# Attention sums moved between engines, centring and decoding split otherwise, in a fused attention and gating kernel

## The chip, the cores and the metric

The kernel runs on one core of one Trainium2 chip. The metric is the device time of one execution in microseconds; the median of the runs is compared. A core has five engines with instruction streams of their own: TensorE (PE) for matrix products, whose weight loads stand in the profile as PEld, VectorE (DVE), ScalarE (ACT), GpSimd (POOL) and SyncE (SP), which issues most of the transfers. The engines wait for each other through semaphores alone.

## The reference

Four batches, twelve heads, 448 positions, 64 columns a head. A capped attention is followed by a block with a gate over positions. Every output has to be there in fp32.

```python
scores = cap * tanh(q @ k.T / sqrt(64) / cap)
attn = exp(scores - max(scores))
attn = attn / (sum(attn) + 1e-09)
x = (attn @ v)                      # heads side by side: 448 x 768
h = gelu_tanh(x @ w_in)             # 768 x 1024
u, v = h[..., :512], h[..., 512:]
v_n = (v - mean(v)) / sqrt(var(v) + 1e-06) * g_ln
v_s = einsum('ts,bsd->btd', w_sg, v_n) + b_sg[None, :, None]
out = x + (u * v_s) @ w_out         # 512 x 768
```

## The kernel before

**Matrix products.** The large products run in a one-pass fp32 format; to keep the precision, each operand is split into a high and a low half, and a product is three matmuls (high times high, high times low, low times high: `TERMS`). Score products use the same split of q and k (`split`, lines 506 and 513), except for head pairs marked in `PLAIN`. The weights come as 64-bit floats and are decoded on the chip, chunk by chunk (`decode`: five steps named low, high, shift, sign and whole, of which the last is an addition on GpSimd, then high and low half).

**Attention.** A batch is three groups of two head pairs. A group has seven units: three key chunks of 128 for each of the two pairs, and one unit with the last 64 keys of both. Each unit is a score step on PE (lines 524, 532, 540), a tanh and an exp on ScalarE (595, 597) and a value step on PE (556, 566). The tiles of exponentials `p` come out of a pool of five, the PSUM tiles of scores `sc` out of two. The denominator, the sum of exponentials over all keys, is made on PE: a matmul against a matrix with one column of ones (`den_op`, line 455) adds a tile of exponentials into the tile `den`. Two units go into one operation of four matmuls. The table `SUMS` says for each of the twelve groups how much VectorE adds up beforehand (`add`, line 608): 0, nothing, and seven units go to PE; 1, the three chunks of each pair are added on VectorE (four additions), and two sums and the tail tile go to PE as three units; 2, the tail tile is added too, in two additions of 64 partitions, and two units are left. After a batch, `recip` sends `den` through DRAM, takes the reciprocal and spreads it; `norm` (675) multiplies the head outputs by it.

**The gated block.** `gated(b)` runs on a finished batch: `hv` (line 729) and `hu` (767) are the two halves of the product with W_in, `vsg` (784) that over positions, `outp` (804) that with W_out. `hv` takes GELU (710 to 717), mean and variance (739, 740), the power -1/2 on GpSimd (743), then the layer norm as one VectorE instruction with two columns, mean and factor (745), and then splits the result into halves (`cop` at 300 or 302, `sub` at 328). The bias (789) multiplies by `g_ln` and adds `b_sg`. `outp` ends with the residual (814) and a store (817).

**Order.** Nothing schedules at run time. Every piece of work is an operation of the class `Plan`; `ORDER` is a table of numbers written out by hand or by a planner, and `Plan.run` emits the operations in that order, so it sets the order on every engine. The last bit of each number chooses the engine where an operation is declared for both VectorE and ScalarE (`BOTH`). PE works on a batch's attention and an earlier batch's gated block by turns.

## Time and profile before

| | |
|---|---|
| median of 3 runs | 376.49 us (376.44 to 376.51) |
| the profiled execution | 376.32 us |
| its span, first to last instruction | 374.5 us |
| busy: PE, VectorE, ScalarE, GpSimd | 369.3, 302.4, 211.6, 39.7 us |
| denominator matmuls (line 455) | 160 records, 19.9 us |
| additions of exponentials (line 608) | 48, 53.9 us |

A busy share is the time in which an engine has at least one instruction running. PE's matmuls overlap, and their ends are modelled, so the starts are what can be read closely: the chain of waits shows each piece from its start to the start of what follows. A matmul in plain fp32 appears as two records, one in the one-pass format as one. VectorE instructions overlap a little too, so the chain's pieces of VectorE are shorter than the mean duration in a group.

### The profile page before, as it was taken

The page shows a single profiled execution, that of the slowest core. Times are in us where ns is not written, and L with a number is a line of the kernel's source. Part 1 is how long each engine was busy: PE and PEld are TensorE (multiplying, and loading weights), DVE is VectorE, ACT ScalarE, POOL GpSimd, SP SyncE. Part 2 cuts the span into 40 slices and gives each one's busy share as a digit, 9 for nine tenths or more (in the row PEclk, how much of TensorE's full clock was granted, in tenths as well). Part 3 has the DMA queues.
Part 4 walks back from the last instruction along what each step waited for, and adds up shares of the span by engine and source line. Part 5 has one row for each costly group of instructions (what it writes and reads, how often), then busy time and mean ns, then how long its engine had stood idle before and what let it go on. Part 6 is the DMA issues. An engine that isn't in the chain of part 4 may idle for free.

```text
span 374.5 us, 5508 instructions
## 1 busy us (share of the span) xinstructions
PE 369.3 (99%) x2064; PEld 251.3 (67%) x2064; DVE 302.4 (81%) x559; ACT 211.6 (56%) x275; POOL 39.7 (11%) x39
## 2 busy tenths in 40 slices
PE   8999999999999999999999999999999999999995
PEld 3334343454877587446478976476889999889995
DVE  2899999999989999989795779889366988438763
ACT  5999999995675758797914377751031411033200
POOL 0321121500311412020000100000001000002000
PEclk9999999999999999999999999999999999999999
DMA  7899164455381245146520021202120101400004
GB/s 264 296 274 309 67 200 139 108 168 149 96 259 44 61 118 194 43 119 201 166 80 2 14 79 42 80 3 78 31 79 24 45 6 51 172 2 0 2 0 172
DMA packets 23130, 39.65 MB, mean 106 GB/s; under 512 B 5472, under 2 KB 17728, under 8 KB 23104
## 3 DMA queue, kind: packets, MB, share of 16 engines
q1 hardware_dynamic: 22816, 38.96, 33.4%
q8 instruction: 16, 0.26, 0.3%
q10 hardware_dynamic: 288, 0.34, 0.3%
q14 instruction: 10, 0.08, 0.1%
HBM read 33.28 MB, written 6.02 MB: 105 GB/s over the span
## 4 chain that ended last, share of the span: by engine, by line
PE 82%; DVE 9%; DMA 3%; ACT 2%; issue 2%; SPq 1%; DVEq 0%; ACTq 0%
PE ps L556 12%; PE ps L767 11%; PE ps L729 10%; PE ps L804 10%; PE sc L524 9%; PE ps L784 8%; PE sc L804 6%; PE den L455 3%; PE sc L767 3%; DMA n<-spread 3%; PE sc L729 2%; PE sc L532 2%; PE ps L566 2%; DVE p L608 2%; SPq L320 1%
## 5 line engine op out<-in xcount | busy, mean ns | idle before, releaser
L597 ACT ACTIVATE p<-p,cap 128x896 f32<-128x896 f32 x84 | 84.8, 1040 | 0.7
L595 ACT ACTIVATE p<-sc 128x896 f32<-128x896 f32 x63 | 56.5, 912 | 15.8 <-DVE p L608 7.1
L556 PE MATMUL ps<-p,v 128*64 128x448 f32 x288 | 61.3, 551 | 0.0
L608 DVE TENSOR_TENSOR p<-p,p 128x896 f32<-128x896 f32 (+1 forms) x48 | 53.9, 1132 | 5.1 <-PE ps L556 2.7
L729 PE MATMUL ps<-winv,rg 128*128 128x512 f32 x205 | 50.8, 394 | 0.0
L524 PEld LDWEIGHTS sc<-hl 64*128 64x128 f32 x378 | 32.7, 185 | 26.0 <-ACT p L595 11.9
L767 PE MATMUL ps<-rg,winu 128*128 128x448 f32 x223 | 49.7, 363 | 0.0
L524 PE MATMUL sc<-hl 64*128 64x448 f32 x378 | 48.5, 384 | 0.0
L767 PEld LDWEIGHTS ps<-rg,winu 128*128 128x128 f32 x223 | 41.8, 188 | 4.0 <-issue 0.7
L729 PEld LDWEIGHTS ps<-winv,rg 128*128 128x128 f32 x205 | 38.5, 188 | 8.6 <-issue 0.7
L400 POOL TENSOR_TENSOR stage<-stage 128x512 int32<-128x512 int32 (+1 forms) x20 | 30.2, 1513 | 113.5 <-DVE stage L395 58.8
L556 PEld LDWEIGHTS ps<-p,v 128*64 128x64 f32 x288 | 17.5, 136 | 34.1 <-issue 21.9
L710 ACT ACTIVATE t<-ps 128x448 f32<-128x448 f32 (+1 forms) x25 | 14.2, 566 | 45.6 <-PE ps L729 29.5
L804 PE MATMUL ps<-rg,wout 128*128 128x448 f32 x166 | 39.4, 366 | 0.0
L804 PEld LDWEIGHTS ps<-rg,wout 128*128 128x128 f32 x166 | 30.8, 188 | 5.0 <-issue 2.7
L784 PE MATMUL ps<-wsg,rg 128*128 128x448 f32 x130 | 30.4, 367 | 0.0
L715 ACT ACTIVATE t<-t 128x448 f32<-128x448 f32 (+1 forms) x30 | 18.0, 602 | 21.5 <-DVE t L712 21.5
L743 POOL TENSOR_TENSOR sm<-sm,pw 128x1 f32<-128x1 f32 x14 | 8.7, 627 | 186.8 <-DVE sm L741 177.4
L784 PEld LDWEIGHTS ps<-wsg,rg 128*128 128x128 f32 x130 | 24.0, 188 | 3.8 <-issue 1.0
L712 DVE SCALAR_TENSOR_TENSOR t<-t,ps 128x448 f32<-128x448 f32 (+1 forms) x25 | 16.2, 649 | 12.6 <-ACT t L710 12.4
L804 PE MATMUL sc<-rg,wout 128*128 128x448 f32 x98 | 24.1, 363 | 0.0
L595 ACT ACTIVATE p<-sc,qsc 128x896 f32<-128x896 f32 x21 | 20.9, 1005 | 4.8 <-PE den L455 1.6
(117 smaller groups left out, 469.0 us busy)
## 6 DMA issues: line engine op xcount, KB each, us to landing
raw<-in_qk_dram SPq DMA_DIRECT2D x22, 448.0 KB
stage<-in_w_in_dram SPq DMA_DIRECT2D x12, 512.0 KB
n<-spread SPq DMA_DIRECT2D x24, 224.0 KB
out_dram<-x SPq DMA_DIRECT2D x23, 224.0 KB
v<-in_vp_dram SPq DMA_DIRECT2D x24, 192.0 KB
stage<-in_w_out_dram SPq DMA_DIRECT2D x8, 384.0 KB
u<-in_w_sgT_dram SPq DMA_DIRECT2D x4, 224.0 KB
vt<-in_vt_dram SPq DMA_DIRECT2D x12, 64.0 KB
```

Source lines behind the costliest of these rows:

```text
L400: nc.gpsimd.tensor_tensor(out=a.bitcast(I32), in0=a.bitcast(I32), in1=hi, op=ALU.add)
L524: nc.tensor.matmul(out=sc.t[:, h, :S], lhsT=hl[s].t[rows, w, 1, 128 * c - 128:128 * c], rhs=hl[s].t[rows, m, 0], start=(k == 0), stop=(k = ...
L556: nc.tensor.matmul(out=pav[s].t[64 * h:64 * h + 64, :S], lhsT=v[s].t[:, 128 * (c - 1) + 64 * h:128 * (c - 1) + 64 * h + 64], rhs=p.t[:, h, ...
L595: op(name("tanh", s, c), "act", c_act(2 * S, True, raw_scores), lambda p=p, sc=sc, r=raw_scores: nc.scalar.activation(out=p.t, in_=sc.t[:, ...
L597: op(name("exp", s, c), "act", c_act(2 * S, False, True), lambda p=p: nc.scalar.activation(out=p.t, in_=p.t, func=ACTF.Exp, scale=cap_sb), ...
L608: op(name("add", s, t), "dve", c_tt(2 * S), lambda: nc.vector.tensor_tensor(out=a.t[rows], in0=a.t[rows], in1=p.t[rows], op=ALU.add), rd=[ ...
L712: op(tag + " cube", "dve", c_tt(n), lambda: nc.vector.scalar_tensor_tensor(out=view(), in0=view(), scalar=1.0 / GELU_A, in1=src(), op0=ALU ...
L715: op(tag + " tanh", "act", c_act(n), lambda: nc.scalar.activation(out=view(), in_=view(), func=ACTF.Tanh, scale=GELU_C * GELU_A), wr=[sq])
L729: nc.tensor.matmul(out=ps.t[:, :HF], lhsT=(xl if a else xh)[c].t[:, t * 128:t * 128 + 128], rhs=win[w][1][:, c, :], start=(c == 0 and k == ...
L767: nc.tensor.matmul(out=ps.t[:, :S], lhsT=win[w][0][:, c, f * 128:(f + 1) * 128], rhs=(xl if a else xh)[c].t[:, :S], start=(c == 0 and k == 0),
L784: nc.tensor.matmul(out=ps.t[:, :S], lhsT=(vl if a else vh)[c].t[:, f * 128:(f + 1) * 128], rhs=wsg[w][:, c, :], start=(c == 0 and k == 0), ...
L804: nc.tensor.matmul(out=ps.t[:, :S], lhsT=wout[w][:, f, c * 128:(c + 1) * 128], rhs=(gl if a else gh)[f].t[:, :S], start=(f == 0 and k == 0 ...
```

## The change

- `SUMS`: group 4 goes from 0 to 1, groups 5, 6 and 7 from 1 to 2. (A further value, 3, gets code and is not used.)
- The layer norm becomes two steps. `center` subtracts the mean and multiplies by -1; it may run on VectorE or ScalarE and needs the mean alone. The factor is applied where the halves are made (`both`): the high half is the centred tile times the factor column, on VectorE or ScalarE, and the low half is the same product minus the high half, in one VectorE instruction. The bias multiplies by the negated `g_ln` (`gneg`, made once), which undoes the -1.
- The decoding step high may run on ScalarE too.
- The stores of the pairs in `LANES` (the last of batch 2 and five of batch 3) are issued in two halves.
- The bias tile lies between the v columns of W_in and W_sg in SBUF; some small tiles move.
- `ORDER` is a new table.

```diff
-SUMS = (0, 1, 1, 1, 0, 1, 1, 1, 2, 2, 2, 2)
+SUMS = (0, 1, 1, 1, 1, 2, 2, 2, 2, 2, 2, 2)
+LANES = (17, 18, 19, 20, 21, 22)
 ORDER = (
-    14, 0, 336, 338, 340, 344, 6, 342, 4, 10, 8, 16, 348, 350, 2, 32, 420, 358, 352, 360, 372, 364, 366, 354, 380, 18,
+    16, 0, 338, 340, 342, 344, 6, 346, 4, 10, 8, 18, 422, 352, 2, 34, 350, 360, 354, 50, 366, 362, 374, 368, 356, 382,
...
+    bsg_sb = wp.tile([128, S], FP32, name="bsg_sb")
+    wsg = [wp.tile([128, NC, S], FP32R, name=f"wsg{w}") for w in range(2)]
...
+    op("gneg", "dve", 0.15, lambda: nc.vector.tensor_scalar(
+        out=gneg, in0=g_sb, scalar1=-1.0, scalar2=None, op0=ALU.mult), rd=[k_const], wr=[k_neg])
...
-        def high_bits():
+        def high_bits(e):
             _, hi, a = words()
-            nc.vector.tensor_scalar(out=a, in0=f32(hi), scalar1=2.0 ** -112, scalar2=None, op0=ALU.mult)
+            if e == "dve":
+                nc.vector.tensor_scalar(out=a, in0=f32(hi), scalar1=2.0 ** -112, scalar2=None, op0=ALU.mult)
+            else:
+                nc.scalar.activation(out=a, in_=f32(hi), func=ACTF.Copy, scale=2.0 ** -112)
...
-            op(name("layernorm", t), "dve", 0.55, lambda: nc.vector.tensor_scalar(
-                out=vv(), in0=vv(), scalar1=sm.t[:, 6:7], scalar2=sm.t[:, 0:1],
-                op0=ALU.subtract, op1=ALU.mult), rd=[sm], wr=[v2])
+            def center(e):
+                if e == "dve":
+                    nc.vector.tensor_scalar(
+                        out=vv(), in0=vv(), scalar1=sm.t[:, 6:7], scalar2=-1.0, op0=ALU.subtract, op1=ALU.mult)
+                else:
+                    nc.scalar.activation(out=vv(), in_=vv(), func=ACTF.Identity, scale=-1.0, bias=sm.t[:, 6:7])
+
+            def both(tag, rows, hi, lo, rd, wr_hi, wr_lo):
+                def high(e):
+                    if e == "dve":
+                        nc.vector.tensor_scalar(out=hi(), in0=v2.t[rows, :HF], scalar1=sm.t[rows, 0:1], scalar2=None, op0=ALU.mult)
+                    else:
+                        nc.scalar.activation(out=hi(), in_=v2.t[rows, :HF], func=ACTF.Copy, scale=sm.t[rows, 0:1])
...
+                op("%d v%s lo %d" % (b, *tag), "dve", c_tt(HF) + 0.06, lambda: nc.vector.scalar_tensor_tensor(
+                    out=lo(), in0=v2.t[rows, :HF], scalar=sm.t[rows, 0:1], in1=f32(hi()), op0=ALU.mult, op1=ALU.subtract),
...
-                out=tt.t[:, :S], in0=ps.t[:, :S], scalar=g_sb[:, f:f + 1], in1=bsg_sb, op0=ALU.mult, op1=ALU.add),
-               rd=[ps, k_const, k_bsg], wr=[tt])
+                out=tt.t[:, :S], in0=ps.t[:, :S], scalar=gneg[:, f:f + 1], in1=bsg_sb, op0=ALU.mult, op1=ALU.add),
+               rd=[ps, k_neg, k_bsg], wr=[tt])
...
-                op(name("store", c) + "ab"[n], eng, ISSUE, lambda sl=sl, queue=queue: queue.dma_start(
-                    out=outT[b, c][:, sl], in_=x.t[:, sl]), rd=[(x, sl.start)], size=128 * cols * 4)
+                parts = 2 if not last and b * KD + c in LANES else 1
+                for m in range(parts):
+                    sm = slice(sl.start + cols * m // parts, sl.start + cols * (m + 1) // parts)
+                    op(name("store", c) + "abc"[n + m + (parts > 1)], eng, ISSUE, lambda sl=sm, queue=queue: queue.dma_start(
+                        out=outT[b, c][:, sl], in_=x.t[:, sl]), rd=[(x, sl.start)], size=128 * cols // parts * 4)
```

Three places show what the new table does. Lines of the changed program are higher by about ten: 556, 524, 532, 455 on PE are 566, 534, 542, 465 there, and 506, 513, 608 on VectorE are 516, 523, 618.

On PE, in batch 1, where the second group (group 4) ends and the third begins. Before, tiles of exponentials go to the denominator one by one:

```order
L524 MATMUL sc0_132<-hl1_90 128x448 x6
L524 MATMUL sc1_133<-hl0_89 128x448 x6
L455 MATMUL den_146<-p2_98,const_sb_79 32x448 x2
L455 MATMUL den_146<-p1_97,const_sb_79 32x448 x2
L532 MATMUL sc0_132<-raw1_87 64x448 x2
L532 MATMUL sc0_132<-raw2_88 64x448 x2
L455 MATMUL den_146<-p0_96,const_sb_79 32x448 x2
L455 MATMUL den_146<-p3_99,const_sb_79 32x448 x2
L524 MATMUL sc1_133<-hl0_89 128x448 x6
L524 MATMUL sc0_132<-hl0_89 128x448 x6
```

The same place now:

```order
L534 MATMUL sc1_134<-hl0_90 128x448 x6
L542 MATMUL sc0_133<-raw1_88 64x448 x2
L542 MATMUL sc0_133<-raw2_89 64x448 x2
L566 MATMUL ps1_136<-p3_100,v0_92 64x448 x2
L566 MATMUL ps1_136<-p4_101,v0_92 64x448 x2
L534 MATMUL sc1_134<-hl0_90 128x448 x6
L465 MATMUL den_147<-p0_97,const_sb_80 32x448 x2
L465 MATMUL den_147<-p2_99,const_sb_80 32x448 x2
L534 MATMUL sc0_133<-hl0_90 128x448 x6
```

One operation of the denominator stands here instead of two; the tiles it reads are sums that VectorE has made.

On VectorE, at about the same place, from the reciprocal of batch 0 (the tile `d`) on. Before:

```order
L641 SCALAR_TENSOR_TENSOR d0_145<-d0_145,guard_70 64x84
L644 RECIPROCAL d0_145<-d0_145 64x84
L395 SCALAR_TENSOR_TENSOR stage3_83<-stage3_83 128x512
L395 SCALAR_TENSOR_TENSOR stage1_81<-stage1_81 128x512
L300 CAST winv0_71<-stage2_82 128x512
L386 TENSOR_SCALAR stage0_80<-stage0_80 128x512
L513 SCALAR_TENSOR_TENSOR hl0_89<-raw1_87,root_69,hl0_89 128x832
L300 COPY x7_108<-ps2_136 128x448
L390 TENSOR_SCALAR stage0_80<-stage0_80 128x512
L328 TENSOR_TENSOR winv1_72<-stage2_82,winv0_71 128x512
```

Now:

```order
L664 RECIPROCAL d0_146<-d0_146 64x84
L516 TENSOR_SCALAR hl0_90<-raw1_88,root_70 128x832
L618 TENSOR_TENSOR p0_97<-p0_97,p4_101 128x896
L523 SCALAR_TENSOR_TENSOR hl0_90<-raw1_88,root_70,hl0_90 128x832
L405 SCALAR_TENSOR_TENSOR stage2_83<-stage2_83 128x512
L516 TENSOR_SCALAR hl1_91<-raw2_89,root_70 128x832
L618 TENSOR_TENSOR p0_97<-p0_97,p1_98 128x896
L400 TENSOR_SCALAR stage1_82<-stage1_82 128x512
L303 CAST winu0_63<-stage0_81 128x512
L303 COPY x8_110<-ps0_135 128x448
L618 TENSOR_TENSOR p2_99<-p2_99,p3_100 128x896
L618 TENSOR_TENSOR p2_99<-p2_99,p4_101 128x896
```

Four additions stand between the reciprocal and the normalisation where decoding stood before.

On VectorE, at the start, after the first scalars. `stage` are the tiles of weights being decoded, `hl` those of the score split. Before:

```order
L513 SCALAR_TENSOR_TENSOR hl0_89<-raw1_87,root_69,hl0_89 128x832
L380 TENSOR_SCALAR stage0_80<-stage0_80 128x512
L386 TENSOR_SCALAR stage1_81<-stage1_81 128x512
L386 TENSOR_SCALAR stage0_80<-stage0_80 128x512
L390 TENSOR_SCALAR stage0_80<-stage0_80 128x512
L395 SCALAR_TENSOR_TENSOR stage0_80<-stage0_80 128x512
L506 TENSOR_SCALAR hl1_90<-raw2_88,root_69 128x832
```

Now:

```order
L523 SCALAR_TENSOR_TENSOR hl0_90<-raw1_88,root_70,hl0_90 128x832
L394 TENSOR_SCALAR stage0_81<-stage0_81 128x512
L387 TENSOR_SCALAR stage0_81<-stage0_81 128x512
L400 TENSOR_SCALAR stage0_81<-stage0_81 128x512
L405 SCALAR_TENSOR_TENSOR stage0_81<-stage0_81 128x512
L516 TENSOR_SCALAR hl1_91<-raw2_89,root_70 128x832
L523 SCALAR_TENSOR_TENSOR hl1_91<-raw2_89,root_70,hl1_91 128x832
L394 TENSOR_SCALAR stage1_82<-stage1_82 128x512
```

The first instruction on the second weight chunk (`stage1`) has moved from ahead of the rest of the first chunk to behind it and behind the next score split.

## Rows read from the trace of the kernel before

**Rows 1.** The page's first part: busy us (share of the span) and instructions of each engine.

```profile
PE 369.3 (99%) x2064; PEld 251.3 (67%) x2064; DVE 302.4 (81%) x559; ACT 211.6 (56%) x275; POOL 39.7 (11%) x39
```

**Rows 2.** Busy time by stretch: length, each engine, clock, DMA share, GB/s.

```profile
60.00:80.00 20.00, 20.00 (x148) 8.14 (x144) 19.21 (x28) 19.52 (x22) 6.77 (x4) 1.00 0.39 103
80.00:100.00 20.00, 20.00 (x101) 12.43 (x98) 19.50 (x36) 12.41 (x19) 1.31 (x1) 1.00 0.48 154
```

**Rows 3.** What PE waited for: us in total, times, longest.

```profile
PE ps L355 <- PEq L891: 0.8, 1, 0.8
```

**Rows 4.** Chain of waits, PE pieces: start, us until the next, line, records.

```profile
10.18 0.89 PE den L455 x8
...
12.49 0.90 PE ps L556 x4
...
17.72 1.65 PE ps L556 x8
19.37 1.43 PE sc L524 x12
20.80 1.64 PE den L455 x16
...
32.50 0.80 PE sc L524 x6
```

**Rows 5.** Chain of waits from 44 to 112 us, VectorE pieces.

```profile
75.75 0.53 DVE x L300
...
76.81 0.34 DVE winu L300
...
78.82 0.30 DVE r L300
79.12 1.01 DVE p L608
...
90.55 0.56 DVE hl L506
...
92.14 1.00 DVE hl L513
93.14 0.54 DVE rg L328
93.68 0.53 DVE wsg L328
```

**Rows 6.** PE in order of time, 80 to 104 us: start, us, records.

```profile
90.08 5.09 PE L729 MATMUL ps<-winv,rg 128*128 128x512 f32 x21
95.00 0.62 PE L729 MATMUL ps<-winv,r 128*128 128x512 f32 x2
```

**Rows 7.** What VectorE waited for up to 130 us.

```profile
DVE stage L386 <- DMA stage<-in_w_in_dram: 2.7, 2, 1.8
DVE hl L506 <- DMA raw<-in_qk_dram: 2.3, 1, 2.3
```

**Rows 8.** VectorE groups by shape: busy us, mean ns, idle before.

```profile
L608 DVE TENSOR_TENSOR p<-p,p 128x896 f32<-128x896 f32 x40 | 45.2, 1142 | 0.8 <-PE ps L556 0.3
...
L745 DVE TENSOR_SCALAR t<-t,sm 128x512 f32<-128x512 f32 x14 | 7.7, 557 | 2.2 <-POOL sm L743 2.1
...
L300 DVE CAST rg<-t 128x512 fp32r<-128x512 f32 x11 | 4.6, 421 | 0.2
```

**Rows 9.** ScalarE groups by shape: the tanh of the GELU.

```profile
L715 ACT ACTIVATE t<-t 128x512 f32<-128x512 f32 x14 | 8.8, 631 | 12.8 <-DVE t L712 12.8
```

**Rows 10.** VectorE in order of time, 50 to 64 us: one addition.

```profile
53.01 2.20 DVE L608 TENSOR_TENSOR p<-p,p 128x896 f32<-128x896 f32 x1
```

**Rows 11.** GpSimd in order of time, 44 to 64 us: the addition of a decoding.

```profile
52.57 1.68 POOL L400 TENSOR_TENSOR stage<-stage 128x512 int32<-128x512 int32 x1 [5.52 <-DVE stage L390]
```

**Rows 12.** Stores on SP: ns min/median/max, first and last start.

```profile
L817 SPq DMA_DIRECT2D out_dram<-x x24: 332/422/570, 160.3 to 371.4; - x24
```

**Rows 13.** Chain of waits from 366 us: the last matmuls, the last residual.

```profile
368.83 1.82 PE sc L804 x9
370.65 0.02 issue
370.67 0.39 DVE x L814
```

More of the change, by code (lines that the diff above doesn't have):

```diff
@@ L250, in tiles, with small @@
         return [wp.tile(shape, dtype, name=f"{name}{i}") for i in range(n)]
-    win = [[wp.tile([128, KD, HF], FP32R, name=f"winu{w}")] for w in range(2)]
-    wout = tiles(2, [128, KF, DM], FP32R, "wout")
-    cap_sb = wp.tile([128, 1], FP32, name="cap")
-    qsc = wp.tile([128, 1], FP32, name="qsc")
-    root = wp.tile([128, 1], FP32, name="root")
-    guard = wp.tile([128, 1], FP32, name="guard")
-    for w in range(2):
-        win[w].append(wp.tile([128, KD, HF], FP32R, name=f"winv{w}"))
-    wsg = tiles(2, [128, NC, S], FP32R, "wsg")
+    def small(n, name):
+        return wp.tile([128, n], FP32, name=name)
+    win = [[None, None], [None, None]]
+    for w in range(2):
+        win[w][0] = wp.tile([128, KD, HF], FP32R, name=f"winu{w}")
+    wout = [wp.tile([128, KF, DM], FP32R, name=f"wout{w}") for w in range(2)]
+    gneg, cap_sb, qsc, root = small(KF, "gneg"), small(1, "cap"), small(1, "qsc"), small(1, "root")
+    for w in range(2):
+        win[w][1] = wp.tile([128, KD, HF], FP32R, name=f"winv{w}")
+    bsg_sb = wp.tile([128, S], FP32, name="bsg_sb")
+    wsg = [wp.tile([128, NC, S], FP32R, name=f"wsg{w}") for w in range(2)]
     sms = tiles(4, [128, 8], FP32, "sm")
@@ L445, in attention @@
         per = {}
-        total = sum((NU, 3, 2)[s] for s in SUMS[NG * b:NG * b + NG])
+        total = sum((NU, 3, 2, 1)[s] for s in SUMS[NG * b:NG * b + NG])
         def den_op(units):
@@ L622, in group, with fold @@
                     add(per[s], p, c)
+                if SUMS[g] == 3:
+                    if c == FC:
+                        def fold(s=s, src=per[s], dst=per[0]):
+                            nc.vector.tensor_tensor(
+                                out=dst.t[64 * s:64 * s + 64], in0=src.t[:64], in1=src.t[64:], op=ALU.add)
+                        op(name("fold", s), "dve", c_tt(2 * S), fold, rd=[per[s]], wr=[per[0]], fast=True)
+                    if (s, c) == (1, FC):
+                        add(per[0], tail_p, 0)
+                        den_unit(pairs[0], 1, per[0], last)
+                    continue
                 if SUMS[g] == 2 and (c == 0 or (s, c) == (1, 1)):
@@ L738, in hv @@
             sm = Buf(sm_p)
-            op(name("stats", t), "dve", 0.69, lambda: nc.vector.bn_stats(out=sm.t[:, 0:6], in_=vv()), rd=[v2], wr=[sm])
-            op(name("mean", t), "dve", 0.18, lambda: nc.vector.bn_aggr(out=sm.t[:, 6:8], in_=sm.t[:, 0:6]), wr=[sm])
+            op(name("stats", t), "dve", 0.69, lambda: nc.vector.bn_stats(out=sm.t[:, 0:6], in_=vv()), rd=[v2], wr=[(sm, "r")])
+            op(name("mean", t), "dve", 0.18, lambda: nc.vector.bn_aggr(out=sm.t[:, 6:8], in_=sm.t[:, 0:6]),
+               rd=[(sm, "r")], wr=[(sm, "m")])
@@ L755, in hv @@
                 mine, other = slice(TL * n, TL * n + TL), slice(TL - TL * n, 2 * TL - TL * n)
[L756 to L758 removed]
+                both((" tail", n), mine, lambda h=h, m=mine: h.t[m], lambda h=h, o=other: h.t[o], [v2], (h, 0), (h, 1))
         uu = {}
```

27 lines of the change are left out of this document (14 added, 13 removed), and 156 rows, old and new, of the table ORDER.

## The prediction

> **What bounds the kernel now.** I read the engines' shares first, then busy time by stretch, then what TensorE's idle time was, and then the chain of waits for the price of each kind of work. TensorE (PE) is busy 369.3 of 374.5 us, VectorE (DVE) 81% [rows 1]. A busy share alone does not say that PE is the bound, so the next views matter more: in the stretches the granted clock is 1.00, PE has no idle time from 60 to 100 us [rows 2], and the largest idle wait of PE in the whole span is 0.8 us, ahead of its first instruction [rows 3]. The chain of waits gives the distance from one start to the next, and this distance is the same each time: a lone denominator operation (eight records, four matmuls) takes 0.89 us and two in a row 1.64, so 0.75 each and 0.14 for entering that kind of work; a lone value step 0.90 and two 1.65, so 0.75 and 0.15; score steps 0.80 and 1.43, so 0.63 and about 0.18 [rows 4]. With such fixed distances the stream of PE is a sum that can be written down, and what is taken out of it shortens the end by as much, provided that the other engines still deliver in time. That proviso is the second half of the reading: VectorE is busy 19.2 and 19.5 of 20 us from 60 to 100, ScalarE 19.5 of 20 from 60 to 80 [rows 2]. In the first half PE is dense because VectorE just keeps up.
>
> The Trainium skill, "Perfetto Trace Analysis", section Identifying the Most-Contended Engine, says that matmul busy time is a poor measure and that the share of weight loads should be looked at. By it the 67% of PEld would mean that PE has room, and the time would stay where it is. The fixed distances in [rows 4] speak against that here; the rival is priced below.
>
> **What leaves PE.** A denominator unit is one tile of exponentials that PE sums over its partitions; two units make one operation. Per group of two head pairs SUMS 0, 1, 2 means 7, 3, 2 units. Batch 0 stays at 7+3+3 = 13 units; batch 1 goes from 3+7+3 = 13 to 3+3+2 = 8; batch 2 from 3+3+2 = 8 to 2+2+2 = 6; batch 3 stays at 6. In operations (an odd unit costs one by itself): 7+7+4+3 = 21 before, 7+4+3+3 = 17 after. Four leave: 4 x 0.75 = 3.00 us, and 4 x 0.89 = 3.56 if each stood alone [rows 4].
>
> **What the new order adds to PE.** I counted in both programs how often PE enters a kind of work: scores 35 before and 37 after, values 32 and 35, denominators 18 and 16; tails and plain scores are unchanged. That is 2 x 0.18 + 3 x 0.15 - 2 x 0.14 = +0.53 us. All other matmuls are the same in number and size. Net on PE: -3.00 + 0.53 = **-2.47 us**.
>
> **What VectorE gets.** Ten more additions, 48 to 58 (the four of group 4, and two half-partition ones each in groups 5, 6, 7), 1.01 us each by distance [rows 5]. Against that seven of 14 centrings, five of 21 high halves of the score splits and nine decoding steps go to ScalarE, so over the whole run VectorE's work grows by only 1 or 2 us. But the place decides. I take the last low half of batch 0's normalised activations, the row at 93.14 us [rows 5], which the first projection (hv) waits for. Counting the VectorE instructions ahead of it in both programs: 6 more additions (+6.06), one score split less (-0.56 - 1.00), two evacuations of PSUM less (-1.06), two decoding steps and one high half of W_in less, of one size (3 x 0.34 = -1.02), two high halves of the activations more (+0.60), and two chunks of W_sg split now on VectorE (+0.60 + 1.06) [rows 5]. Sum **+4.7 us** of work ahead of that instruction, while PE's stream up to the same matmul is about as long as before: three of the four removed operations stood ahead of it, but two plain score steps of batch 2 and some projection steps now do.
>
> How much of this has cover? In the kernel before, the low half ends at 93.7. The projection run of PE starts at 90.08 [rows 6]; 21 of its matmuls take 4.92 us up to the next row's start at 95.00, 0.23 each; six steps of three stand ahead of the step that reads the low half in its third matmul, (18 + 2) x 0.23 = 4.6, so it is wanted at about 94.7: 1.0 us of slack. Second, VectorE waited 2.7 us for two W_in loads early on [rows 7], and the new order has a score split and the rest of chunk 0 in those places, so I count these 2.7 us as regained. The 2.3 us for the first qk load [rows 7] stay; its second half is issued one place earlier, ahead of a v load, which gains at most one issue. 4.7 - 1.0 - 2.7 = **1.0 us** by which PE waits. Bounds: nothing, if the rest is absorbed too; 3.7, if nothing of the early waits is regained. I take 1.0.
>
> Centring now needs only the mean, not the power that GpSimd computes; that takes the short wait on GpSimd out of VectorE's way in front of the centring, and puts it in front of the high half. The high half on VectorE now takes the factor from a column: between a cast of that size, 421 ns, and the centring with two such columns, 557 ns [rows 8]; ten of them, so 0 to 1.4 us, only half of them before 130 us. I take the upper price, and it stays inside the bounds above. A centring on ScalarE lies near its 631 ns for a tile of that size [rows 9]. From 80 us on ScalarE has gaps (12.4 of 20 us busy) [rows 2], which cover the centrings at no cost; before 80 us it has next to none, and gets a few decoding steps, each of which makes an exponential later by its own length. I count that into the same bounds. The negated gain column is one column wide; the bias tile's new address changes no instruction: both at nothing, and the rows show no time that hangs on an address.
>
> **GpSimd beside the additions.** A 2.20 us addition instead of 1.14 stands in the trace, beside a GpSimd addition of 1.68 us that began 0.44 us before it [rows 8, 10, 11]. GpSimd has the same 20 decoding additions in both programs, so I add nothing for it.
>
> The Trainium skill, "SBUF — State Buffer", says that a VectorE instruction with two SBUF inputs and a GpSimd instruction that reads SBUF exclude each other, and the later one blocks for the whole of the other. The pair in [rows 10, 11] agrees. By that rule the loss goes by the number of GpSimd instructions, not of additions, and the sum keeps its zero; read from the row alone, each of the ten additions could lose 1.1 us, and the sum would come out slower than before.
>
> **The end.** Six stores of the end become twelve; an issue on SP takes 0.33 to 0.57 us, median 0.42 [rows 12]. After the matmuls of the last whole residual (c = 1), PE still has four steps of three matmuls, 0.20 each (2.4 us) [rows 13], and SP has four or five halves to issue (1.7 to 2.1), so the queue is just free when the last residual is done. Taken at 0; bounds -0.3 (less data in flight behind the last store) and +0.6.
>
> **Sum.** The profiled execution took 376.32 us with a span of 374.5; the median is 376.49. -2.47 + 1.0 = -1.47: span 373.0, and against the median **375.0 us**.
>
> **Rivals.** (a) *VectorE fully keeps up*: no wait arises, 376.49 - 2.47 = 374.0; with 3.56 for the four operations 373.5 (-3.56 + 0.53). For it: the order was rebuilt around the new work, and centring has left VectorE's chain. Against: VectorE busy 19.5 of 20 us. (b) *VectorE is late, slower than before*: the additions of groups 4 and 5 hold tiles of exponentials (five buffers) and stand ahead of the normalisation of batch 0 and of the next score splits; if the early waits come back in another place, PE waits 4.7 - 1.0 = 3.7 us, 376.49 - 2.47 + 3.7 = 377.7. It turns slower from 2.47 us of PE waits. For it: [rows 2] and the 1.0 us of slack. (c) *The change does not reach the end*: what leaves PE comes back as waits of the same size, or PE had room all along; 376.5. (d) *The end grows*: SP's queue holds the last store back by 0.6 on top of the forecast, 375.6.
>
> **How the numbers follow.** Forecast 0.45, (a) 0.18, (b) 0.20, (c) 0.09, (d) 0.08. A change of 0.2% (0.75 us) is about what a measurement here can tell from none: faster below 375.74, slower above 377.24. The forecast (374.2 to 375.9) gives 0.41 faster and 0.04 same; (a) is faster; (b), spread from 376.5 to 378.2, gives 0.15 slower and 0.05 same; (c) 0.01 faster, 0.07 same, 0.01 slower; (d) 0.02 faster, 0.06 same. Together 0.62, 0.22, 0.16. The range leaves out half of (b) and the edge of (a): 373.6 to 377.4.
>
> **What would show it.** In the trace of the changed kernel the denominator's records should fall from 160 to 132, each lone operation still 0.89. PE's starts should be as evenly spaced as now, with one or two holes between 60 and 150 us that end with VectorE, about 1 us in all; VectorE's early wait on W_in loads should be gone. Holes of 3 us or more, or ScalarE waiting on additions for its tiles, is (b); no hole is (a). The end now comes 3.8 us after the start of the last residual at 370.67 [rows 13]; over 4.2 us is (d). I am wrong if denominators cost less than 0.75 each when removed, or if holes arise late, after 200 us, where I see room.

## The result, and the profile after

The changed kernel takes **372.9 us** (median of six runs, 372.07 to 373.46) against 376.47 us of the kernel before beside it (six runs, 375.23 to 376.67): ratio 0.991, 95% interval 0.9892 to 0.9927, 3.6 us less. The direction was forecast, the size was not: 375.0 was the forecast time, and 373.6 the lower end of the range.

The page's first part of the kernel after, as in [rows 1]: busy us, share of the span, instructions.

```profile
PE 365.8 (99%) x2036; PEld 250.1 (67%) x2036; DVE 304.7 (82%) x548; ACT 224.2 (60%) x297; POOL 37.2 (10%) x39
```

PE is 3.5 us shorter and as dense as before; VectorE has 2.3 us more work and ScalarE 12.6 us more. The stretches of [rows 2] in the kernel after (length, busy time of each engine, clock, DMA share, GB/s):

```profile
60.00:80.00 20.00, 20.00 (x139) 8.09 (x135) 19.74 (x30) 19.76 (x25) 2.72 (x2) 1.00 0.48 146
80.00:100.00 20.00, 19.67 (x96) 12.47 (x95) 19.53 (x33) 15.59 (x22) 3.53 (x2) 1.00 0.37 102
```

All three engines are full from 60 to 80 us. The largest change in that stretch is GpSimd's: 2.72 us where [rows 2] have 6.77. What PE waited for in the whole span of the kernel after, as [rows 3] (us in total, times, longest):

```profile
PE ps L362 <- PEq L931: 0.8, 1, 0.8
PE sc L550 <- ACT p L605: 0.4, 1, 0.4
PE ps L804 <- DVE t L737: 0.3, 1, 0.3
```

And what VectorE waited for up to 130 us, as [rows 7], the first three of the list:

```profile
DVE cap L338 <- DMA first_sb<-in_first_dram: 3.6, 1, 3.6
DVE hl L516 <- DMA raw<-in_qk_dram: 2.0, 1, 2.0
DVE p L618 <- ACT p L607: 0.7, 1, 0.7
```

The 2.7 us for W_in of [rows 7] are gone; the 2.3 us for the first qk load are 2.0. The denominator operations in the group view (records, then busy us and mean ns), and one of them in order of time (start, us):

```profile
L465 PE MATMUL den<-p,const_sb 128*32 128x448 f32 x132 | 16.1, 550 | 0.0
```

```profile
62.18 0.96 PE L465 MATMUL den<-p,const_sb 128*32 128x448 f32 x8
63.07 0.98 PE L576 MATMUL ps<-p,vt 64*64 64x448 f32 x8
```

132 records instead of 160, and from this one's start to the next step 0.89 us, the price of [rows 4].

**Where the 3.4 us of the span come from.** I wrote down PE's stream of both kernels as the sum of its steps at fixed distances: for attention those of [rows 4], for a projection step of three matmuls 0.60 us ([rows 13]; 0.69 where a matmul takes 0.23, [rows 6]). What the trace takes beyond that sum is holes (the start and usual entries into projection runs are among them, in both kernels).

| us | before | after | difference | forecast |
|---|---|---|---|---|
| PE's stream as a sum | 363.93 | 361.48 | -2.45 | -2.47 |
| holes of PE | 5.77 | 4.93 | -0.84 | +1.0 |
| rest of the span | 4.85 | 4.74 | -0.11 | 0 |
| span | 374.55 | 371.15 | -3.40 | -1.47 |

(The rest is what lies ahead of PE's first matmul, 0.77 in both, and behind its last.) So one line of the forecast failed, that of the holes.

Two cautions. The first line is a count: the forecast and the sum take the same steps times the same distances, so their agreement says that the steps were counted rightly. What a step is worth in time is shown by runs below. And one part of the holes changes from run to run by itself: PE's first twelve score records, from 4.0 us on, take 3.1 to 4.3 us in the traces of these runs (3.40 before, 3.45 after).

### The profile page after: what moved, and what is told of

It is laid out like the page before. It is cut to its first block, busy times and chain, and to the rows that moved or that the text cites. A ratio compares the mean times of both kernels' runs of the same rounds, so it can differ in the third digit from the quotient of the medians.

```text
span 371.2 us, 5490 instructions
## 1 busy us (share of the span) xinstructions
PE 365.8 (99%) x2036; PEld 250.1 (67%) x2036; DVE 304.7 (82%) x548; ACT 224.2 (60%) x297; POOL 37.2 (10%) x39
## 4 chain that ended last, share of the span: by engine, by line
PE 86%; DVE 8%; ACT 2%; DMA 2%; issue 1%; DVEq 0%; ACTq 0%
PE ps L566 14%; PE ps L804 12%; PE sc L534 11%; PE ps L841 11%; PE ps L749 8%; PE ps L821 5%; PE sc L841 5%; PE sc L749 4%; PE sc L804 4%; PE den L465 4%; PE ps L576 2%; PE sc L542 2%; PE sc L821 2%; DVE p L618 2%; DMA n<-spread 2%; PE sc L550 1%
## 5 line engine op out<-in xcount | busy, mean ns | idle before, releaser
L618 DVE TENSOR_TENSOR p<-p,p 128x896 f32<-128x896 f32 (+1 forms) x58 | 64.1, 1107 | 5.1 <-PE ps L566 3.5
L804 PE MATMUL ps<-rg,winu 128*128 128x448 f32 x206 | 46.5, 363 | 0.0
L841 PE MATMUL ps<-rg,wout 128*128 128x448 f32 x180 | 44.8, 365 | 0.0
L749 PE MATMUL ps<-winv,rg 128*128 128x512 f32 x170 | 43.1, 394 | 0.0
L804 PEld LDWEIGHTS ps<-rg,winu 128*128 128x128 f32 x206 | 38.5, 188 | 3.4 <-issue 0.3
L749 PEld LDWEIGHTS ps<-winv,rg 128*128 128x128 f32 x170 | 31.8, 188 | 7.5 <-issue 1.0
L841 PEld LDWEIGHTS ps<-rg,wout 128*128 128x128 f32 x180 | 33.4, 188 | 4.8 <-issue 1.0
L821 PE MATMUL ps<-wsg,rg 128*128 128x448 f32 x116 | 26.7, 365 | 0.0
L730 ACT ACTIVATE t<-sc 128x512 f32<-128x512 f32 (+1 forms) x8 | 4.5, 572 | 35.6 <-PE sc L749 32.7
L523 DVE SCALAR_TENSOR_TENSOR hl<-raw,root,hl 128x832 fp32r<-128x832 f32 x21 | 24.0, 1143 | 0.1
```

What stands on the lines that cost most here:

```text
L523: op(name("qk lo", s), "dve", c_tt(n) + 0.06, lambda: nc.vector.scalar_tensor_tensor(out=used(hl[s].t[:, 1]), in0=used(raw[s].t), scalar=r ...
L618: op(name("add", s, t), "dve", c_tt(2 * S), lambda: nc.vector.tensor_tensor(out=a.t[rows], in0=a.t[rows], in1=p.t[rows], op=ALU.add), rd=[ ...
L749: nc.tensor.matmul(out=ps.t[:, :HF], lhsT=(xl if a else xh)[c].t[:, t * 128:t * 128 + 128], rhs=win[w][1][:, c, :], start=(c == 0 and k == ...
L804: nc.tensor.matmul(out=ps.t[:, :S], lhsT=win[w][0][:, c, f * 128:(f + 1) * 128], rhs=(xl if a else xh)[c].t[:, :S], start=(c == 0 and k == 0),
L821: nc.tensor.matmul(out=ps.t[:, :S], lhsT=(vl if a else vh)[c].t[:, f * 128:(f + 1) * 128], rhs=wsg[w][:, c, :], start=(c == 0 and k == 0), ...
L841: nc.tensor.matmul(out=ps.t[:, :S], lhsT=wout[w][:, f, c * 128:(c + 1) * 128], rhs=(gl if a else gh)[f].t[:, :S], start=(f == 0 and k == 0 ...
```

## The experiments

The question is what made PE's stream count in full, and why VectorE did not add holes. Theory 1: in the kernel before, PE's stream and its suppliers VectorE and ScalarE are equally late, so a shorter stream helps only if the suppliers get time too. Rivals: VectorE alone sets the pace, or VectorE had room all along.

### The sums apart from the order

**The new kernel with the old sums.** SUMS goes back, the ten additions and their four denominator operations with it; everything else stays in the new order.

```
-SUMS = (0, 1, 1, 1, 1, 2, 2, 2, 2, 2, 2, 2)
+SUMS = (0, 1, 1, 1, 0, 1, 1, 1, 2, 2, 2, 2)
...  (ORDER: without the ten additions, with four more denominator operations)
```

> The changed kernel with the old SUMS: ten additions fewer, 21 denominator operations again, the rest of the new order and engines kept. PE's stream is 3.86 us longer by the fixed distances (four operations at 0.75, four more entries into denominators, two into values, one into the W_out product's stretch). Theory 1: 372.9 + 3.9 = 376.8, or 0.7 less if the remaining holes close. Rival 2: as the changed kernel or faster, 372.9 or less, since VectorE has 10 us less to do. Rival 3: as theory 1.

Measured: 376.95 us, 1.002 of before (1.0012 to 1.0029), 4.05 us over the kernel after. PE's sum grows by 3.86; its holes fall by 0.4, all of it in the first score steps. The gain is the shorter stream, and the new order alone, with its additional entries, is even a little slower than the old one.

**The old kernel with the new sums.** The same edit the other way round; the ten additions stand where their inputs are ready, the old order is kept otherwise.

> The kernel before with the new SUMS alone: ten more additions, 17 instead of 21 denominator operations, each put in as soon as its inputs stand in the old order; everything else keeps its place and engine. By the fixed distances of the rows PE's stream is 2.75 us shorter. Theory 1 (the end is PE's stream, VectorE just keeps up, and the new order made room for the additions): the old order has no room, VectorE's 4.7 us minus 1.0 of slack come back as holes on PE, 376.5 to 377.7. Rival 2 (VectorE alone sets the pace): 378 or more. Rival 3 (VectorE had room all along, any order would do): 373.7.

Measured: 399.69 us, ratio 1.0631 (1.0613 to 1.065): 23 us slower, a miss of every theory. PE's sum is 361.18, as short as in the kernel after; the holes take 31.8 us. What PE waited for in it, the two largest:

```profile
PE sc L524 <- ACT p L595: 4.4, 5, 2.4
PE ps L556 <- ACT p L597: 3.8, 2, 3.2
```

and ScalarE (the product tiles p are the exponentials' tiles):

```profile
ACT p L595 <- DVE p L608: 20.2, 11, 4.8
```

The same wait in the kernel before and in the kernel after:

```profile
ACT p L595 <- DVE p L608: 7.1, 7, 1.9
```

```profile
ACT p L605 <- DVE p L618: 2.1, 3, 1.6
```

An addition that comes late holds tiles that ScalarE needs for the next tanh, and PE waits for ScalarE. Ten additions are 10 us of VectorE's time, and PE's holes grew by 26: most of the price lies in where the additions stand, not in their 1.0 us each.

**The old kernel without the four denominator operations**, nothing in their place (three of batch 1, one of batch 2).

```
             def fn():
+                if (b, n0) in ((1, 2), (1, 4), (1, 8), (2, 2)):
+                    return
                 for half, (p, kind, src) in enumerate(units):
```

> The kernel before without four of its denominator operations (three in batch 1, one in batch 2), whose sums are left out; no addition takes their place. PE's stream is 3.6 us shorter (3.00 and four entries). Theory 1: PE now outruns VectorE, which has not less to do, and gets holes; 1.0 us of slack and the old holes mean 374.5 to 375.5. Rival 2: 376.5. Rival 3: 372.9.

Measured: 376.44 us, ratio 0.9999 (0.9985 to 1.0012). PE's sum is 3.6 us shorter and its holes are 3.6 us longer: 0.7 us of that in the first score steps, which vary by themselves, 2.2 us between 63 and 73 us and 0.8 us at 141 us. This kernel from 60 to 80 us and 140 to 160 us, and PE's waits for ScalarE, four in all, which lie in these two stretches:

```profile
60.00:80.00 20.00, 18.61 (x126) 7.55 (x124) 19.33 (x29) 19.80 (x23) 6.98 (x4) 1.00 0.37 108
140.00:160.00 20.00, 19.61 (x121) 12.02 (x119) 19.69 (x39) 16.46 (x21) 2.06 (x2) 1.00 0.37 116
```

```profile
PE sc L526 <- ACT p L597: 1.3, 3, 0.5
PE ps L558 <- ACT p L599: 0.4, 1, 0.4
```

From 60 to 80 us ScalarE is busy 19.8 of 20, and PE, freed of its sums, stands before the next score or value step until ScalarE has made a tile free or an exponential ready. In the old list the denominators filled time in which PE would otherwise have waited for ScalarE.

**The new kernel with four denominator operations made twice**, on the same inputs.

```
-                for half, (p, kind, src) in enumerate(units):
+                twice = (b, n0) in ((1, 2), (1, 4), (2, 2), (3, 2))
+                for half, (p, kind, src) in enumerate(units + units if twice else units):
```

> The changed kernel with four denominator operations made twice in place (two in batch 1, one each in batches 2 and 3), so those sums count double. Four times 0.75 us on PE, no new entry, nothing else. Theory 1 and rival 3: 372.9 + 3.0 = 375.9, or down to 375.3 if the 0.7 us of holes that are left close behind it. Rival 2: 372.9.

Measured: 376.22 us, 3.3 over the kernel after, ratio to before 1.0 (0.9991 to 1.0008). Each took 1.64 us instead of 0.89 from start to start, as here:

```profile
62.49 1.71 PE L466 MATMUL den<-p,const_sb 128*32 128x448 f32 x16
64.14 0.98 PE L577 MATMUL ps<-p,vt 64*64 64x448 f32 x8
```

After the change four operations of PE cost their 3.0 us in full; before it, taking four away gives nothing. PE is the bound after; before, PE and ScalarE were late together.

### Is it the first 25 microseconds?

**Three VectorE instructions of the old kernel a few places later** (the high words of W_in's chunks 1.1 and 0.0, and 0.0's low words), past work whose data are there.

```
-in 1.1 high, in 0.1 high, in 0.1 shift, in 0.1 sign
+in 0.1 high, in 0.1 shift, in 0.1 sign, in 1.1 high
-in 0.0 high, in 4.1 low, in 0.0 low, in 4.1 sign
+in 4.1 low, in 4.1 sign, in 0.0 high, in 0.0 low
```

> Kernel of before in which three VectorE instructions of W_in's decoding stand a few places later (the high words of chunks 1.1 and 0.0 and the low words of 0.0, behind work whose data have landed), so that VectorE's two early waits for W_in (1.8 and 0.9 us) shrink by about 2.3 us; nothing else is changed. Theory 1 (VectorE and PE are both tight in batch 0, and PE's stream of 363.9 us stays): only the holes that VectorE leaves in PE go, 1.66 us by my list of them, so 0.5 to 1.5 us less than before, 374.7 to 375.9 us. Rival (VectorE's backlog is the bound, as the third hypothesis of the prediction had it): all 2.3 us, 374 us. Rival (regained time is worth nothing before the PE stream is shorter): 376.2 to 376.5 us.

Measured: 376.25 us, ratio 0.9992 (0.998 to 1.0004), and inconclusive: the waits moved to the instructions behind, instead of going away (2.4 us for W_in in two rows of the same view, and 1.0 us for a PSUM tile that PE had not written yet).

```profile
DVE stage L386 <- DMA stage<-in_w_in_dram: 1.8, 2, 1.1
DVE x L300 <- PE ps L566: 1.0, 1, 1.0
DVE stage L380 <- DMA stage<-in_w_in_dram: 0.6, 1, 0.6
```

**The old kernel with the first 25 us of the new list** on all engines, loads too, the old order behind it.

```
-(order of before, up to the low halves of qk of chunk pair 5)
+(order of after for these instructions, then before's for the rest)
```

> Kernel of before, in which only the first 25 us follow the new list (loads, decoding and scores up to the low halves of qk of chunk pair 5, on every engine), everything behind it stands in the old order; nothing is added or left out. VectorE's early waits for W_in (2.7 us) should go. Theory 1 (PE and VectorE are both tight in batch 0): PE can win only the holes that VectorE leaves in it, 375.0 to 376.0 us. Rival (VectorE alone is late in the kernel before): 373.8 us. Rival (the early waits were no loss): 376.3 us.

Measured: 375.56 us, ratio 0.9977 (0.9965 to 0.9989). The wait for W_in (2.7 us) is gone from VectorE's list, and 0.6 us reach the end.

**The same, and without the four denominator operations.**

```
 (the order above)
+                if (b, n0) in ((1, 2), (1, 4), (1, 8), (2, 2)):
+                    return
```

> The same kernel, and the four denominator operations of batches 1 and 2 that were left out alone before (three of chunk group 1, one of group 2; their part of the denominators is missing) left out here too. Alone, neither the shorter PE stream nor, by theory 1, the regained VectorE time brings much; theory 1: together they bring most of the 3.0 us of PE work, 373.0 to 374.5 us. Rival (the room comes from later places of the new list, not from its first 25 us): 376.0 to 376.5 us, as with the four operations left out alone.

Measured: 376.14 us, ratio 0.9993 (0.9981 to 1.0006). Theory 1 in the form "VectorE's early waits give the room" falls. PE still waits for ScalarE in the same places, by the same amount. (The profiled execution, 374.96 us, is the fastest of the twelve; PE's holes in it are 2.2 us longer than before, not 3.6, and the median has no gain.)

```profile
60.00:80.00 20.00, 18.62 (x126) 7.60 (x122) 18.44 (x27) 19.48 (x23) 5.67 (x4) 1.00 0.42 120
```

```profile
PE sc L526 <- ACT p L597: 1.3, 3, 0.5
PE ps L558 <- ACT p L599: 0.4, 1, 0.4
```

VectorE has 1.6 us to spare in this stretch, and PE has its holes nevertheless. What turns the shorter stream into time is the later part of the new list, with the split of work that belongs to it. By the traces it sends PE to the first projection 2.2 us sooner (82.14 us before, 79.95 after), with part of the scores behind it, so that PE has other work where it would stand before ScalarE; and ScalarE is busy 19.81 and 19.89 of 20 us from 20 to 60, where it was 19.11 and 19.11. That these two differences do it is argued, not shown, and which of its moves does most was not taken apart.

### How much room VectorE has

**One VectorE instruction at about 20 us executed four times**, +2.0 us, in the old and in the new kernel.

```
+                        for _ in range(4 if name("qk hi", s) == "0.4 qk hi" else 1):
                             nc.vector.tensor_scalar(
```

> Kernel of before in which one VectorE instruction at about 22 us (the high halves of qk of chunk pair 4 of batch 0) is executed four times: 2.0 us more for VectorE at a place where the scores that read it are 5 us away, the same result. Theory 1: VectorE has less than 1 us of room against PE up to 93 us, so the end moves by 1 to 2 us, 377.3 to 378.3 us. Rival (2 us of room): 376.3 us.

> Kernel after with the same instruction executed four times, at about 20 us. Theory 1 (the new list regained about 5 us of VectorE's time and spent 4.65 us of it on the added sums, so that it has as little room as the kernel before): 1 to 2 us over 372.9, that is 373.9 to 374.9 us. Rival (the regained time left room of 2 us or more): 372.9 us.

Measured: old 376.81 us (ratio 1.0014, 1.0005 to 1.0022), 0.5 us of 2.0; new 374.16 us, 1.3 of 2.0. The old kernel swallows 1.5 us: 1.1 by 32 us (its waits for W_in fall from 2.7 to 1.3), and most of the rest in PE's hole at 104.92 us. The new kernel has less room than the old one, so it is not the case that VectorE merely had time to spare after the change.

**One addition executed five times** (+4 us) at about 60 us, in the old and in the new kernel.

```
+                    times = 5 if name("add", s, t) == "1.1 add 3" else 1
+                    op(name("add", s, t), "dve", c_tt(2 * S), lambda: [nc.vector.tensor_tensor(
+                        out=a.t[rows], in0=a.t[rows], in1=p.t[rows], op=ALU.add) for _ in range(times)],
...
```

> Kernel of before in which one 896-column addition of batch 0 (group 3 of pair 1, the one that closes that sum) is executed five times, so that VectorE has four additions of about 1.0 us more and every product of the sum is counted with a wrong weight; PE's work is the same. Theory 1 (VectorE and ScalarE were as tight as PE in batch 0 of the kernel before): all of it becomes a hole of PE, 376.5 + 3 to 4 = 379.5 to 380.5 us. Rival (VectorE had some 4 us to spare there): 376.5 to 377.5 us. What lies between says how much of 4 us the order of before could swallow.

> Kernel after with the same addition executed five times (four more VectorE instructions of about 1.0 us in batch 0, a wrong weight in the sum). Theory 1 (the new list lost its early waits for W_in and so regained more of VectorE's time than its added work took): some room is left, a part of 4 us is swallowed, 374 to 376 us, and the loss is smaller than that in the kernel before. Rival (as much room as before, the gain is the shorter PE stream alone): the loss against 372.9 is as large as that of the kernel before against 376.5, 376 to 377 us.

Measured: old 381.29 us (+5.1), new 379.22 us (+6.3), both more than the work added. The addition closes a sum that PE's next denominator operation reads, so PE stood until it was done, and the experiment says less about room than meant. PE in the new kernel with it, and two stretches (the number behind POOL's is the granted clock):

```profile
66.73 1.72 PE L465 MATMUL den<-p,const_sb 128*32 128x448 f32 x8 [3.58 <-DVE p L619]
68.38 1.77 PE L576 MATMUL ps<-p,vt 64*64 64x448 f32 x8
```

```profile
60.00:70.00 10.00, 6.42 (x36) 1.77 (x34) 9.86 (x14) 5.78 (x7) 1.29 (x1) 0.75 0.12 46
70.00:80.00 10.00, 10.00 (x66) 4.57 (x64) 8.87 (x12) 8.90 (x12) 1.42 (x1) 0.91 0.52 141
```

A hole of 3.6 us, and behind it the lone denominator takes 1.65 us instead of 0.89, the tail's value step 1.70 instead of 0.91 and the two score steps after it 2.17 instead of 1.42. The granted clock of 0.75 in this stretch is a mix of its two levels (1.2 and 2.4 GHz). Of the loss, 2.3 us are these slower steps.

**The new kernel without its ten additions.**

```
+                    skip = g == 4 or g in (5, 6, 7) and not t
-                    op(name("add", s, t), "dve", c_tt(2 * S), lambda: nc.vector.tensor_tensor(
+                    op(name("add", s, t), "dve", c_tt(2 * S), lambda: skip or nc.vector.tensor_tensor(
```

> Kernel after without its ten added sums on VectorE: those additions are left out (the columns that they would have summed are missing from the denominators), about 10.5 us less for VectorE, and PE's stream stays as it is. Theory 1 (after, PE's stream is the bound and 4.9 us of waits and usual starts are left of which under 1 us can be VectorE's): 372.0 to 372.9 us. Rival (VectorE is the bound after): 3 to 10 us less, 363 to 370 us.

Measured: 371.72 us, ratio 0.9886 (0.987 to 0.9901), 1.2 us less for 10.5 us of VectorE work; PE's holes fall from 4.93 to 3.70. From 60 to 80 us VectorE is now busy 15.2 of 20, and PE is as dense as with them:

```profile
60.00:80.00 20.00, 20.00 (x139) 8.25 (x136) 15.20 (x27) 19.75 (x25) 2.83 (x3) 1.00 0.50 146
```

The additions' whole price after the change is thus 1.2 us.

**The new kernel with centring, high halves and high words on VectorE** (the 22 steps of these kinds that ScalarE had), each in its place.

```
-(step, "act")   22 steps: centring and high halves of v (13), high words of decodings (9)
+(step, "dve")
```

> Kernel after with all 22 steps of centring, v's high half and decoding that stand on ScalarE executed on VectorE, each in the place where it stood; nothing is left out. VectorE gets about 14 us more over the run, ScalarE as much less, PE's stream is unchanged. Theory 1 (VectorE is as tight as PE through long stretches, so the split of this work is what makes the sums fit): holes of PE of 3 to 10 us, 376 to 383 us, which takes the gain away. Rival (the split is not needed, VectorE has room for it): 372.9 to 374 us.

Measured: 378.04 us, ratio 1.005 (1.0036 to 1.0063), 5.1 over the kernel after; PE's holes grow from 4.93 to 10.0, nearly all between 89 and 180 us. The other split is a condition of the gain.

### GpSimd beside VectorE

**The new kernel with five of GpSimd's additions made twice**, VectorE and PE with the same work.

```
+            if tag in ("in 3.1 ", "in 4.1 ", "in 5.1 ", "in 2.0 ", "in 3.0 "):
+                nc.gpsimd.tensor_tensor(out=lo, in0=a.bitcast(I32), in1=hi, op=ALU.add)
             nc.gpsimd.tensor_tensor(out=a.bitcast(I32), in0=a.bitcast(I32), in1=hi, op=ALU.add)
```

> Kernel after in which GpSimd executes five of its 1.4 us additions of W_in's decoding twice (chunks 3.1, 4.1, 5.1, 2.0 and 3.0, at 28 to 70 us; the first execution goes into words that nobody reads, the result is the same). VectorE and PE have no more work. Theory 1 (part of what the new list regained is VectorE time that was lost beside GpSimd: before 75 us an instruction of GpSimd costs VectorE about 0.6 us on average, and after has fewer of them in that stretch): five more cost VectorE 2 to 4 us and move the end by 1 to 3 us, 374 to 376 us. Rival (GpSimd beside VectorE costs nothing that reaches PE): 372.9 us.

Measured: 376.81 us, 3.9 over the kernel after; 7.8 us of GpSimd's time take the whole gain. VectorE's additions between 25 and 80 us in the kernel before, after, and in this one (count, then busy us and mean ns):

```profile
L608 DVE TENSOR_TENSOR p<-p,p 128x896 f32<-128x896 f32 x13 | 16.3, 1257 | 0.4 <-PE ps L556 0.3
```

```profile
L618 DVE TENSOR_TENSOR p<-p,p 128x896 f32<-128x896 f32 (+1 forms) x19 | 21.2, 1118 | 1.5 <-ACT p L607 0.7 <-PE ps L566 0.6
```

```profile
L620 DVE TENSOR_TENSOR p<-p,p 128x896 f32<-128x896 f32 x16 | 22.9, 1431 | 1.5 <-ACT p L609 1.3
```

An undisturbed addition takes 1.09 us, as the one at 37.07 us below. So the old list loses 13 x 0.17 = 2.2 us in this one group, the new list 19 x 0.03 = 0.5, and this kernel 16 x 0.34 = 5.5. One meeting, VectorE and then GpSimd of this kernel in order of time (start, us):

```profile
36.88 1.14 DVE L303 COPY x<-ps 128x448 f32<-128x448 f32 x2
37.94 0.73 DVE L405 SCALAR_TENSOR_TENSOR stage<-stage 128x512 int32<-128x512 int32 x1
38.60 2.19 DVE L620 TENSOR_TENSOR p<-p,p 128x896 f32<-128x896 f32 x1
```

```profile
36.70 1.43 POOL L411 TENSOR_TENSOR stage<-stage 128x512 int32<-128x512 int32 x1 [4.30 <-DVE stage L400]
38.20 3.75 POOL L412 TENSOR_TENSOR stage<-stage 128x512 int32<-128x512 int32 x2
```

The two copies out of PSUM run beside GpSimd's first addition at their usual 0.62 us. The addition behind them begins 0.4 us after GpSimd's next and takes 2.19 us, twice its own time.

### The parts put at nothing, and a next step

**The new kernel with whole stores and the bias tile at its old address.**

```
-LANES = (17, 18, 19, 20, 21, 22)
+LANES = ()
-    bsg_sb = wp.tile([128, S], FP32, name="bsg_sb")      (ahead of wsg)
+    bsg_sb = wp.tile([128, S], FP32, name="bsg_sb")      (ahead of guard, pw)
```

> Kernel after with whole stores in place of the six in halves, and with the bias tile at its old address; nothing is left out. My sum has both at nothing: 372.7 to 373.2 us. Rival (the stores in halves shorten or lengthen the end): 0.5 us or more either way.

Measured: 373.09 us, ratio 0.9909 (0.9894 to 0.9924): for the two together no difference from the kernel after that can be told.

**The new kernel with one more denominator operation on VectorE**, in batch 3, two additions placed one VectorE instruction behind their inputs.

```
-SUMS = (0, 1, 1, 1, 1, 2, 2, 2, 2, 2, 2, 2)
+SUMS = (0, 1, 1, 1, 1, 2, 2, 2, 2, 3, 3, 2)
...  (ORDER: two additions more, one denominator operation less)
```

> Kernel after in which the sums of two more chunk pairs of the last batch are made on VectorE (two additions of 1.1 us more, one denominator operation less on PE), in the old order otherwise; nothing is left out. Theory 1 (PE's stream is the bound and VectorE has room behind 200 us): PE's sum falls by 0.74 us, 372.1 to 372.4 us. Rival (VectorE has no room there): 372.9 to 374 us.

Measured: 384.57 us, ratio 1.0215 (1.0196 to 1.0234), 11.7 over the kernel after, a miss of both. PE's sum fell by the 0.74 us; its holes grew by 13, between 187 and 263 us. What ScalarE waited for from 180 to 260 us:

```profile
ACT p L605 <- PE ps L566: 9.2, 4, 4.7
ACT p L605 <- DVE p L618: 5.9, 2, 4.6
```

And the longest wait of VectorE there, for a product over positions on PE:

```profile
DVE t L826 <- PE ps L821: 5.5, 2, 4.2
```

It is the mechanism of the old kernel with the new sums: VectorE is busy 10.6 to 15.8 of 20 us from 200 to 260 and has time, and the additions still come too late for the tiles. Up to 236.4 us it stood 4.2 us before a bias step that needs PE, with an addition behind it in its list; ScalarE waited 4.6 us for that addition, and PE for ScalarE. After two of the holes the granted clock fell to 0.57 (191 to 195 us) and 0.62 (246 to 250 us); by the distances of the steps there, about 3 of the 13 us are slower steps, an estimate. No version that beats the kernel after came out of this.

## Why the prediction was wrong

**PE's stream: right.** -3.00 for four operations and +0.53 for entries were forecast, and the new trace has -2.45 by the same distances, with 132 records and 0.89 us for a lone operation. With the old sums the new order gives 3.86 us of the sum back, and 4.05 in time. What the prediction had not seen is that this term is not worth its size by itself: in the old list it is worth nothing, since PE then stands before ScalarE. Its own third rival described that, and the two kernels without the four operations (376.44 and 376.14) are that rival. The busy share of ScalarE from 60 to 80 us, 19.5 of 20, stood in [rows 2], and the prediction drew from it only what moved decoding steps might cost, not that PE would wait for ScalarE once it has less to do.

**VectorE's term: the step that failed.** It was put at 4.7 (work) - 1.0 (slack) - 2.7 (early waits) = +1.0 us of holes; -0.84 was measured. Six additions more, and no wait for W_in, are in the trace. By this sum the last low half, the row at 93.14 us in [rows 5], should have come 2.0 us later. It came 0.3 us earlier, here in order of time in the kernel before and the kernel after:

```profile
93.06 0.62 DVE L328 TENSOR_TENSOR rg<-x,rg 128x448 fp32r<-128x448 f32 x1
```

```profile
92.75 0.61 DVE L331 TENSOR_TENSOR rg<-x,rg 128x448 fp32r<-128x448 f32 x1
```

So the sum had 2.3 us of VectorE's time too much. 1.8 of them are the step on GpSimd: "GpSimd has the same 20 decoding additions in both programs, so I add nothing for it". Up to 92 us both kernels have ten, 17.2 us of them before and 16.0 after. But VectorE lost 7.6 us beside them before and 5.8 after, summed over the instructions that took longer than others of their kind. The other 0.5 is no idle time: apart from W_in, VectorE idles 7.7 us ahead of this row before and 7.8 after. It lies in the work, which by this count grew by 4.3 us and not by 4.7; why is open. That time lost beside GpSimd reaches the end is measured: 7.8 us more of GpSimd's time cost 3.9. No run moved the meetings in the old kernel, so the 1.8 us stand by the count in the two traces.

The Trainium skill, "SBUF — State Buffer", section SBUF: two separate sides, says that a VectorE instruction with two SBUF inputs and a GpSimd instruction that reads SBUF exclude each other for the whole of the one that is first. The prediction drew from it that the loss goes by GpSimd's number. The traces agree with the page (the copies out of PSUM above do not wait, the addition does) and not with what I drew from it: the loss goes by what VectorE has next when GpSimd starts, and that is a matter of order. The old list had two whole additions there, [rows 10] one of them; the new list has copies out of PSUM at 29, 35, 49, 62 and 68 us. The two old meetings cost VectorE 2.2 us, these five 1.3.

**The holes themselves.** Besides the start, the two largest of before are the denominator operation at 54.84 us, 0.5 us late because of the addition in [rows 10], and 0.7 us more than usual in the projection run at 104.92, where PE waits twice for VectorE's last GELU step (line 717). After, there are 0.37 in the run from 89 us on and 0.35 at 142 us. They do lie between 60 and 150 us and end with VectorE, as forecast, but they take the place of larger ones. The 1.2 us that VectorE's additions still cost after the change, by the kernel without them, are near the forecast 1.0 by chance, since that 1.0 was what was left of 4.7 us of work after two other terms. I had set it on top of a kernel that I took for free of holes, since [rows 3] name no wait of PE that ends with VectorE.

**The end: right.** The span ends 3.8 us after the last residual's start, as in [rows 13] (371.15 - 367.38), here in the chain of waits of the kernel after, and whole stores change nothing that can be told:

```profile
364.34 3.02 PE ps L841 x15
367.36 0.02 issue
367.38 0.39 DVE x L851
```

**The rivals.** (a), VectorE keeps up, 374.0, was nearest: its mechanism held, and it left out that holes of the old list go too. (b), ScalarE waiting on additions for its tiles, did not happen in this kernel, whose wait of this kind fell from 7.1 to 2.1 us. It is what happens to the same sums in another order: 399.69. I had this mechanism at 1.2 us over before, and it costs 23. (c) was right for the old list alone. The Trainium skill's rule on weight loads ("Perfetto Trace Analysis", Identifying the Most-Contended Engine), read as room for PE, does not hold after the change: at 67% of PEld, four operations more cost 3.3 us.

## What to carry to other kernels

When every engine is near full, an engine's stream can be summed from its start distances, as here to within 6 us of 375, but what is taken out of the sum is worth its size only where the list gives that engine other work while its suppliers are late; ask of each removed operation what PE's next instruction waits for at that place. Work that is moved to another engine is priced by the buffers it holds and by where it stands, and not by its length alone: the same ten additions cost 1.2 us in one order and 26 us of holes in another. And an engine that holds another up is counted by their meetings, not by its instructions.

## What the runs showed of the hardware that I had not expected

A VectorE instruction between SBUF tiles that comes after the start of a GpSimd addition lasts until about its own length after GpSimd's end (38.60 us above: 2.19 us instead of 1.09), while a copy out of PSUM passes beside it at its usual 0.62 us. An instruction with one full input tile waits too: the high half at 38.08 us below takes 1.70 us, where the one at 93.28 us takes 0.64. These instructions share no tile with GpSimd's, and the time is lost inside them; so the sentence on the chip that engines wait for each other through semaphores alone does not hold for this pair. GpSimd waits in the same way: in the kernel after, its addition that starts at 37.16 us while VectorE adds takes 2.17 us, against 1.41 us of its usual length.

```profile
37.07 1.09 DVE L618 TENSOR_TENSOR p<-p,p 128x896 f32<-128x896 f32 x1
38.08 1.70 DVE L516 TENSOR_SCALAR hl<-raw,root 128x832 fp32r<-128x832 f32 x1
```

```profile
37.16 2.17 POOL L410 TENSOR_TENSOR stage<-stage 128x512 int32<-128x512 int32 x1 [0.65 <-DVE stage L405]
```

After one hole of PE of 3.6 us the granted clock was 0.75 in that stretch of 10 us and 0.91 in the next, which cost another 2.3 us. With one more fold on VectorE a wait of 2.1 us before 190.66 us was followed by 0.57 from 191 to 195 us; in the old kernel with the new sums a wait of 2.4 us before 140.51 us was not (1.00 from 138 to 144 us). In the kernel after, PE's longest wait from 60 to 100 us is 0.3 us, and its stretches here stand at 1.00.
